# RoPE attention and SiLU FFN on one core: the same 2671 parts in another issue order, 516 of them on another engine

## The chip, the cores and the metric

The kernel runs on one core of a Trainium2 chip. The metric is device time in microseconds (us) from launch to end. Before the change three runs took 667.82, 668.82 and 671.1 us, a median of 668.82 us.

## What is computed

Attention over 4 batches, 8 heads, 576 positions and head size 64, with a rotation of q and k by position (RoPE), and a feed-forward network (FFN) on its output, 2304 tokens wide 512, inner width 2048. All inputs are 32-bit floats. Cut to what matters:

```python
q_rot, k_rot = rotate(q), rotate(k)
scores = 1 / sqrt(64) * q_rot @ k_rot.T
attn = exp(scores - max(scores)); attn /= sum(attn) + 1e-9
x = (attn @ v), heads side by side          # 2304 x 512
h = x @ w_in                                # 512 -> 2048
out = (h * sigmoid(h)) @ w_out              # 2048 -> 512
```

## The kernel before, in words

Matmuls run on TensorE (PE) with 16-bit operands. A 32-bit number is held as a high and a low half: the high half is the number times a scale, rounded to 16 bits; the low half is what that rounding left over. So nearly every tensor is made twice on the other engines: a "hi" step (one multiplication; L327 on ScalarE, called ACT, or L321 on VectorE, called DVE, and GpSimd, called POOL) and a "lo" step. On DVE a lo step is one fused instruction (L333); on POOL it is two, a multiplication (L321) and a subtraction (L336). POOL can take neither a score nor any other tile that PE writes, since those lie in PSUM; all its work is between tiles in SBUF.

The work comes in named parts, each a few instructions on one engine:

- For each batch b and pair of heads p: loads of q, k and v (`qld`, `vld`), a scale for each from its sum of squares (`qtr`, `qtd`, `qmm` and `sc0` to `sc2`), three rotation steps for q and for k (`rope`: L471, L475, L478), their halves (`qhi`, `qlo`), the transposes by DMA (`qT`), a copy of K with the halves swapped (`ksw`), and the halves of v (`vhi`, `vlo`).
- For each of 8 slices of the weights: two loads (`wld`), a rewriting of the bits (`wT`, `wC` and `wX`, L651 to L664), a scale (`wtr`, `wtd`, `wmm`), and halves (`whi`, `wlo`).
- For each of 144 slots, a slot being 128 query rows against 576 keys of one head: scores on PE (`S`, L778 and L784, into one of 2 PSUM buffers), the row maximum on DVE (`max`), the exponential on ACT (`exp`, L810), the reciprocal of the row sum (`nr0`, `nr1`), the halves of the probabilities (`hi`, `lo`, written to a tile named `pn`), and a transpose by DMA (`T`, L836). The maximum has two forms: a reduction (L799) with a small negation behind it (`neg`, L805 on ACT or L321 on DVE), or a fused form on DVE (L794 with a read of its accumulator), which needs no negation.
- For each unit (half of a batch's query rows, 8 units) and pair: probabilities times v on PE (`pv`, L875), whose result becomes the halves of the FFN's input (`xh`, `xl`, L893).
- For each unit and weight slice: the first FFN matmuls (`m1`, 24 matmuls, L929), tanh on ACT (L941; L939 in the last), a fused add and multiply on DVE (`g`, L945), halves (`gh`, `gl`), and twice 6 second matmuls (`m2`, L985). The last FFN unit, `rem`, has the query rows left over by the others.

Each part has a list of the engines that it may run on. Nothing else decides the order: a table named `ORDER` (L38 to L168) lists all 2671 parts by number with a letter for the engine (t is PE, a ACT, d DVE, D the fused maximum on DVE, p POOL, s the queue of DMA issues on SyncE, called SP, A a DMA issue from ACT). The program walks it once, and each engine's instructions stand in the order of the walk:

```python
with tc.manual_schedule():
    for z, e in re.findall(r"(\d+)(\w)", ORDER):
        pl.run(pl.names[int(z)], e)
```

The engines work through their own instructions strictly in that order; semaphores make one wait for another. The number of buffers is fixed: three each for the exponentials (`e`), the halves of the probabilities (`pn`) and the FFN inputs (`xh`, `xl`), two for scores, one for `m1` and for `g`, two for `gh` and `gl`.

The two helpers that make the halves, with the choice of engine:

```python
def part_hi(e, hi, src, s):
    if e is act: act.activation(hi, src, AF.Copy, scale=s)
    else: times(e, hi, src, s, 1.0)
def part_lo(e, lo, src, s, hi):
    if e is dve: dve.scalar_tensor_tensor(out=lo, in0=src, scalar=s, in1=hi, op0=ALU.mult, op1=ALU.subtract)
    else:
        times(e, src, src, s, 1.0)
        e.tensor_tensor(out=lo, in0=src, in1=hi, op=ALU.subtract)
```

Of the kernel before, what the change touches and what calls it, by code (L numbers as in the profile page):

```python
# [38 lines left out]
1s 4s 5t 21d 3s 2s 38s 0d 72s 540s 544s 7t 39t 6d 41t 22d 8d 9t 10d 11d 23p 75t 55p 15p 42d 56p 40d 16d 57d 76d 83d  # L39
73t 43t 84d 13d 542a 541a 543d 44d 545a 74d 546p 547d 45d 17p 77t 550t 551d 46d 28s 12d 18p 29t 24a 58d 30d 19d 31t  # L40
96s 130s 78d 79d 80d 32d 49p 33d 20s 50p 62s 47d 25d 51d 26s 34d 89p 90d 548t 97t 98d 549d 85d 552t 553d 27A 59p 52d
53d 35a 99t 100d 36d 54s 86a 87d 63t 106s 61A 131t 101d 744t 91d 37d 14d 60s 102d 560s 92p 745D 753t 64d 93d 132d 754d
133t 134d 746a 103p 747a 748a 88s 749d 755a 105d 756a 735t 736D 48d 65t 117d 554d 66d 135d 109t 107t 140t 555d 750a
110d 108d 141d 136d 751d 752s 564s 762t 737a 738a 763d 739a 556a 764d 104d 765a 766a 94s 586s 123d 740d 741a 767d 557d
111t 757a 758d 771t 118p 772D 742d 137a 119p 112d 773d 138d 113d 562a 774a 558a 142t 789t 143d 114d 759p 120p 790d
124d 81d 115d 760d 566p 125p 780t 568s 561a 791d 792a 743s 781D 768d 769d 559d 144d 67d 563d 798t 799d 782d 770s 139d
68d 565a 567d 775a 126a 587a 127d 116d 569a 783a 784d 570a 761s 606s 571d 69a 70d 800d 793a 794d 785d 786a 95A 121d
787d 574t 572t 776d 777p 795a 788s 147s 573d 575d 576t 122s 577d 801a 796d 71d 578d 579d 807t 580a 778d 2031t 590s
797s 802d 803d 128s 129s 82d 808D 581d 809d 582p 810a 811d 825t 145d 583d 162p 826D 804a 805d 827d 146d 588a 607a 816t
817d 828a 829a 812d 818a 819a 813p 592a 148a 830d 156d 589d 2032d 2033d 814d 834t 806s 779s 835d 820a 591a 630s 608a  # L50
609d 836a 149a 852t 150t 157d 610s 837a 831a 593d 151d 163p 821d 152d 832d 853D 854d 838a 839d 584d 632a 833s 843t
822p 823p 844D 153d 855a 724d 2034t 612a 164d 611a 634s 824s 594t 595d 158p 631a 159p 596t 597d 840d 598t 599d 154d
600d 626s 613d 845a 846a 861t 862d 635a 165a 636a 847a 841d 842s 614t 615d 633d 178s 616t 637d 848d 617d 863a 2035a
864a 618t 849a 856a 585d 815s 627a 160p 850d 601d 865d 619d 620d 857d 870t 871D 640t 851s 858p 628a 187p 629d 859d
2036d 872d 638t 602a 873a 874a 875d 621d 866d 641d 639d 604a 876a 867a 603d 642t 643d 644d 868d 860s 645d 622a 646a
877p 897t 898d 605d 648p 899a 647d 900a 869s 650a 878s 879t 2037t 880d 915t 651d 2038a 881a 882a 672s 888t 623d 901a
883a 624a 884d 2039d 2040t 885p 916D 917d 918a 902d 625d 2041d 906t 919a 889D 920d 903a 652s 674a 2042d 886p 166p 890d
904d 891a 892d 921a 893d 887s 161s 656s 907D 908a 2127t 924t 925D 2128a 909a 2129d 653a 2130a 926d 922d 725d 654a 905s
# [12 lines left out]
1051D 1052d 2165d 697d 1030p 2170d 1053a 1035a 1054a 1021p 1041t 1042d 1036a 720a 2047a 1037d 1059t 1031s 1055d 1043d
176d 2171t 200s 2048d 1038a 718a 2174a 1039d 2049t 1044a 1045a 1056a 1060d 2175d 719d 1022s 1040s 1086t 721p 2176a
1061d 177d 240s 2180t 1046d 1047p 1048p 1057d 2177d 1062a 2050a 201a 1063a 2163d 1058s 1087d 722a 1068t 1064d 1065a
1088d 2172t 1089a 2051d 2181a 202t 1069D 1070d 1071a 1090a 217d 723d 203d 2182d 2178t 1072d 2179t 1104t 204d 727d
1091d 1073d 205d 230A 255p 2183p 1077t 1049s 229s 249d 1078d 206a 241a 207d 1066d 1079d 2052t 1067s 2184p 2185t 208d
231s 1074a 1092a 2053a 1093d 2054d 1105d 1094s 242a 1080a 1075d 2186d 1106a 1107a 2191t 2192a 1081d 1108d 2188t 2193d
250p 1095t 1082d 1076s 2194a 243t 244d 1096D 1097a 1083d 1098a 1113t 2198t 2195d 251p 1109d 245d 246d 252a 1084d 256p
257d 2199a 2200d 2196t 1140t 2189d 1141d 1114D 1085s 258a 1115a 259d 253p 2205t 232a 2187s 233t 234d 2201a 254s 1116a
1099a 1117d 1118d 728d 247d 235d 1100d 1101p 1142d 2202d 1110a 1111d 2197t 1131t 2203t 2204t 236d 1102d 2206a 1143a
2207d 1119d 1122t 262s 2208a 1132D 263a 237p 238d 1133d 1134a 1123d 1120d 1124a 1135d 2212t 239d 1144d 1149t 1136d  # L80
264t 2209p 265d 1150D 1145d 266d 1125a 1126a 260s 1112s 1103s 261A 1137p 2210t 271t 1138d 2211t 272d 1127d 1121s 1128d
273t 274d 2213a 1158t 1151d 2214d 1159D 275d 1129p 1160d 276d 1152a 2055t 1153d 248d 2215d 277d 2216d 1154d 1146a
# [1005 lines left out]
```

## Time and profile before

| what | us |
|---|---|
| median of three runs | 668.82 |
| the profiled execution | 666.31 |
| its span, first to last instruction | 664.5 |
| PE busy | 580.1 (87%) |
| DVE busy | 511.5 (77%) |
| ACT busy | 392.0 (59%) |
| POOL busy | 332.9 (50%) |

A busy time is the time in which at least one instruction of the engine ran. The shares are means over stages that differ: the first 200 us, in which inputs and weights are made ready beside the first slots, and the rest, in which slots and FFN matmuls alternate. The 1.8 us between the profiled time and the span lie before the first and after the last instruction.

### The profile page before, as it was taken

The page shows a single profiled execution, that of the slowest core. Times are in us where ns is not written, and L with a number is a line of the kernel's source. Part 1 is how long each engine was busy: PE and PEld are TensorE (multiplying, and loading weights), DVE is VectorE, ACT ScalarE, POOL GpSimd, SP SyncE. Part 2 cuts the span into 40 slices and gives each one's busy share as a digit, 9 for nine tenths or more (in the row PEclk, how much of TensorE's full clock was granted, in tenths as well). Part 3 has the DMA queues.
Part 4 walks back from the last instruction along what each step waited for, and adds up shares of the span by engine and source line. Part 5 has one row for each costly group of instructions (what it writes and reads, how often), then busy time and mean ns, then how long its engine had stood idle before and what let it go on. Part 6 is the DMA issues. An engine that isn't in the chain of part 4 may idle for free. (4 is left out here: it accounts for less than half of the span.)

```text
span 664.5 us, 12551 instructions
## 1 busy us (share of the span) xinstructions
PE 580.1 (87%) x4428; PEld 382.8 (58%) x4428; DVE 511.5 (77%) x1201; ACT 392.0 (59%) x817; POOL 332.9 (50%) x288
## 2 busy tenths in 40 slices
PE   3463668797889899899989989999999999999997
PEld 2331345564556576656666656666666666666663
DVE  5899999999998989889869889888778976322112
ACT  2156778888877676667774765755556554112322
POOL 4532347346755566833657547746555365231220
PEclk9999766989989999999998999999999999999999
DMA  9799989997898949899994799896865775200201
GB/s 313 144 200 277 250 253 210 193 231 200 144 164 157 181 88 175 146 164 187 167 197 88 124 163 179 157 153 125 181 119 106 89 128 113 53 17 0 49 1 33
DMA packets 233327, 98.34 MB, mean 148 GB/s; under 512 B 214192, under 2 KB 214448, under 8 KB 233264
## 3 DMA queue, kind: packets, MB, share of 16 engines
q1 hardware_dynamic: 232144, 95.47, 72.1%
q10 hardware_dynamic: 1120, 2.07, 1.4%
q8 instruction: 35, 0.57, 0.4%
q14 instruction: 28, 0.23, 0.1%
HBM read 36.16 MB, written 4.72 MB: 62 GB/s over the span
## 5 line engine op out<-in xcount | busy, mean ns | idle before, releaser
L929 PEld LDWEIGHTS <-w_in 128*128 128x128 f16 x1728 | 166.4, 98 | 37.9 <-issue 8.1
L929 PE MATMUL m<-xh,w_in 128*128 128x256 f16 x1024 | 178.7, 273 | 3.2 <-DVE g L945 3.0
L985 PE MATMUL m<-w_out,gh 128*128 128x512 f16 x576 | 173.4, 383 | 0.0
L810 ACT ACTIVATE e<-s,small 128x576 f32<-128x576 f32 x144 | 111.7, 775 | 59.3 <-DVE s L794 15.3
L929 PE MATMUL m<-xl,w_in 128*128 128x256 f16 x512 | 139.5, 273 | 2.1 <-DVE xl L893 2.0
L778 PE MATMUL s<-Tk,Tq 128*128 128x512 f16 (+1 forms) x512 | 90.6, 306 | 26.3 <-ACT e L810 19.6
L985 PE MATMUL m<-w_out,gl 128*128 128x512 f16 x288 | 110.4, 383 | 1.1 <-DVE small L819 0.4
L333 DVE SCALAR_TENSOR_TENSOR pn<-e,small,pn 128x576 f16<-128x576 f32 x105 | 97.2, 926 | 8.6 <-POOL pn L321 4.3
L945 DVE SCALAR_TENSOR_TENSOR g<-g,m 128x512 f32<-128x512 f32 x72 | 49.1, 682 | 70.9 <-ACT g L941 39.4
L985 PEld LDWEIGHTS <-gh 128*128 128x128 f16 x576 | 53.2, 100 | 53.9 <-issue 4.1
L321 POOL TENSOR_SCALAR pn<-e,small 128x576 f16<-128x576 f32 x43 | 40.4, 940 | 83.7 <-DVE small L824 37.4
L941 ACT ACTIVATE g<-m,small 128x512 f32<-128x512 f32 x64 | 43.7, 683 | 62.3 <-PE m L929 50.8
L778 PEld LDWEIGHTS <-Tq 128*128 128x128 f16 x512 | 42.1, 105 | 65.6 <-issue 33.1
L327 ACT ACTIVATE pn<-e,small 128x576 f16<-128x576 f32 x77 | 59.0, 769 | 29.0 <-DVE small L824 11.3
L875 PE MATMUL pv<-pt,vh 128*64 128x256 f16 (+1 forms) x576 | 68.8, 307 | 4.0 <-DMA pt<-pn 2.7
L794 DVE TENSOR_SCALAR_CACHE_REDUCE s<-s,small 128x576 f32<-128x576 f32 x82 | 66.5, 814 | 4.2 <-PE s L778 3.0
L321 POOL TENSOR_SCALAR g<-g,small 128x512 f32<-128x512 f32 x30 | 24.8, 826 | 64.9 <-DVE gh L321 30.7
L336 POOL TENSOR_TENSOR pn<-e,pn 128x576 f16<-128x576 f32 x39 | 55.6, 1425 | 3.3
L985 PEld LDWEIGHTS <-gl 128*128 128x128 f16 x288 | 28.3, 98 | 38.4 <-DVE gl L333 4.0
L875 PEld LDWEIGHTS <-vh 128*64 128x64 f16 x576 | 39.7, 118 | 15.0 <-issue 10.9
L321 POOL TENSOR_SCALAR e<-e,small 128x576 f32<-128x576 f32 x39 | 35.5, 910 | 25.6 <-ACT pn L327 18.7
L799 DVE TENSOR_REDUCE small<-s 128x1 f32<-128x576 f32 x62 | 46.1, 745 | 1.2 <-PE s L778 0.9
(145 smaller groups left out, 933.4 us busy)
## 6 DMA issues: line engine op xcount, KB each, us to landing
out_dram<-ob SPq DMA_DIRECT2D x36, 128.0 KB, 2.5
w_in<-in_moe_w_in_dram SPq DMA_DIRECT2D x4, 1024.0 KB, 6.4
w_out<-in_moe_w_out_dram SPq DMA_DIRECT2D x4, 1024.0 KB, 6.8
io<-in_v_dram SPq DMA_DIRECT2D x13, 288.0 KB, 4.0
io<-in_q_dram SPq DMA_DIRECT2D x13, 288.0 KB, 3.4
io<-in_k_dram SPq DMA_DIRECT2D x13, 288.0 KB, 3.7
io<-in_v_dram SPq DMA_DIRECT2D x13, 256.0 KB, 4.4
ring<-in_moe_w_in_dram SPq DMA_DIRECT2D x3, 1024.0 KB, 7.1
```

Of the source, the lines that this page charges most:

```text
L321: e.tensor_scalar(out=out, in0=in0, scalar1=s1, scalar2=s2, op0=ALU.mult, op1=ALU.bypass if s2 is None else ALU.mult)
L327: act.activation(hi, src, AF.Copy, scale=s)
L333: dve.scalar_tensor_tensor(out=lo, in0=src, scalar=s, in1=hi, op0=ALU.mult, op1=ALU.subtract)
L336: e.tensor_tensor(out=lo, in0=src, in1=hi, op=ALU.subtract)
L778: pe.matmul(o, tq[:, j, 2 * c:2 * c + 2, :], kt[:, r0:r1, js], start=(n == 0), stop=(n == 1))
L794: dve.tensor_scalar(out=t, in0=t, scalar1=cc[:, 1:2], scalar2=None, op0=ALU.mult, op1=ALU.min, accum_out=m_of(1, 2),)
L799: dve.reduce_max(out=m_of(0, 1), in_=buf("s", i)[:, 0:S], axis=AX.X)
L810: act.activation(buf("e", i), buf("s", i)[:, 0:S], AF.Exp, bias=m_of(1, 2), scale=-1.0 if fused[i] else cc[:, 0:1], accum_out=m_of(2, 3),)
L875: pe.matmul(o[64 * j:64 * j + 64, 0:m], vt[part][:, j, s, :], pt[:, a, j, 0:m], start=(z == 0), stop=(z == len(steps) - 1),)
L929: pe.matmul(t[:, c, 0:n], w[:, wz, kk, fs], xx[:, kk, 0:n], start=(kk == 0 and x == 0), stop=(kk == KD - 1 and x == 2),)
L945: dve.scalar_tensor_tensor(out=g, in0=g, scalar=1.0, in1=t, op0=ALU.add, op1=ALU.mult)
L985: pe.matmul(o, gs[gz][:, c, ts], w[:, wz, c], start=(first and c == 0 and x == 0), stop=(last and c == 1 and x == 2),)
```

## The change

Only the table `ORDER` changes. The parts, their code, their tiles and buffers are the same. Its first line, as an example:

```diff
-1s 4s 5t 21d 3s 2s 38s 0d 72s 540s 544s 7t 39t 6d 41t 22d 8d 9t 10d 11d 23p 75t 55p 15p 42d 56p 40d 16d 57d 76d 83d
...
+45d 50p 55d 545a 12d 73t 74d 18a 24a 19d 51p 75t 83d 25p 541a 29t 30d 76d 542a 77t 56d 78d 79d 20s 47d 13d 46d 96s 57d
```

On PE the sequence of parts keeps its pattern and changes by a few places here and there. Over the whole program 516 parts run on another engine than before. What that sums to, in numbers of parts:

| part | before | after |
|---|---|---|
| `lo` of the slots, DVE / POOL | 105 / 39 | 95 / 49 |
| `qlo`, DVE / POOL | 25 / 7 | 21 / 11 |
| `gh`, ACT / DVE / POOL | 35 / 23 / 14 | 38 / 15 / 19 |
| `gl`, DVE / POOL | 42 / 30 | 41 / 31 |
| `rope`, DVE / POOL | 42 / 54 | 47 / 49 |
| `vhi`, ACT / DVE / POOL | 10 / 2 / 4 | 5 / 7 / 4 |
| `whi`, ACT / DVE / POOL | 17 / 1 / 2 | 19 / 0 / 1 |
| maximum, reduction / fused | 62 / 82 | 50 / 94 |
| `nr0`, ACT / DVE | 84 / 60 | 75 / 69 |
| `ksw`, issued by ACT / SP | 7 / 9 | 3 / 13 |

The first place is on POOL, in the preparation of batch 0, whose q, k and v lie for the time being in the weights' tiles `w_in` and `w_out` (and whose halves lie in `n` or `w_out`). Before:

```order
L478 TENSOR_TENSOR w_in<-w_in,rt 128x576
L321 TENSOR_SCALAR n<-w_in,small 128x9x64
L471 TENSOR_TENSOR rt<-w_out,sin_t 128x576
L475 TENSOR_TENSOR w_out<-w_out,cos_t 128x576
L471 TENSOR_TENSOR rt<-w_in,sin_t 128x576
L321 TENSOR_SCALAR w_out<-w_out,small 128x576
L336 TENSOR_TENSOR w_out<-w_out 128x9x64
L321 TENSOR_SCALAR w_out<-w_in,small 128x9x64
L321 TENSOR_SCALAR vh<-w_in,small 128x1152
```

And after, on the same engine, from the fifth instruction of the preparation on:

```order
L321 TENSOR_SCALAR w_in<-w_in,small 128x576
L336 TENSOR_TENSOR n<-w_in,n 128x9x64
L321 TENSOR_SCALAR w_out<-w_out,small 128x576
L336 TENSOR_TENSOR w_out<-w_out 128x9x64
L471 TENSOR_TENSOR rt<-w_in,sin_t 128x576
L475 TENSOR_TENSOR w_in<-w_in,cos_t 128x576
L478 TENSOR_TENSOR w_in<-w_in,rt 128x576
L471 TENSOR_TENSOR rt<-io,sin_t 128x576
L321 TENSOR_SCALAR vh<-w_in,small 128x1152
L321 TENSOR_SCALAR w_in<-w_in,small 128x576
L336 TENSOR_TENSOR w_out<-w_in,w_out 128x9x64
```

Where POOL had one low half (the L321 and L336 in a row), it now has three in this stretch and a fourth right behind it; the two single L321 on `n` and `w_out`, high halves, have gone to ACT.

The second place is on DVE, around the low half of the FFN input of unit 1's last pair (`xl`, L893), for which the first FFN matmul of unit 1 waits. Before:

```order
L799 TENSOR_REDUCE small<-s 128x1
L333 SCALAR_TENSOR_TENSOR vl_130<-io,small,vh 128x320
L333 SCALAR_TENSOR_TENSOR pn<-e,small,pn 128x576
L321 TENSOR_SCALAR small<-small 128x1
L333 SCALAR_TENSOR_TENSOR vl_130<-io,small,vh 128x320
L333 SCALAR_TENSOR_TENSOR pn<-e,small,pn 128x576
L893 SCALAR_TENSOR_TENSOR xl<-pv,small,xh 128x256
L893 SCALAR_TENSOR_TENSOR x_rem_122<-pv,small,x_rem_121 128x64
L799 TENSOR_REDUCE small<-s 128x1
L333 SCALAR_TENSOR_TENSOR pn<-e,small,pn 128x576
```

And after:

```order
L333 SCALAR_TENSOR_TENSOR vl_130<-io,small,vh 128x320
L824 RECIPROCAL small<-small 128x1 x2
L794 TENSOR_SCALAR s,small<-s,small 128x576
L333 SCALAR_TENSOR_TENSOR pn<-e,small,pn 128x576
L333 SCALAR_TENSOR_TENSOR vl_130<-io,small,vh 128x320
L893 SCALAR_TENSOR_TENSOR xl<-pv,small,xh 128x256
L893 SCALAR_TENSOR_TENSOR x_rem_122<-pv,small,x_rem_121 128x64
L794 TENSOR_SCALAR s,small<-s,small 128x576
L819 TENSOR_SCALAR small<-small 128x1
```

Both reductions (L799) have become fused maxima (L794), the negation between them is gone, and one low half of the probabilities (`pn`) fewer stands ahead of `xl`.

## Rows read from the trace of the kernel before

**Rows 1.** The page: the span, and each engine's busy time, share and instructions.

```profile
span 664.5 us, 12551 instructions
PE 580.1 (87%) x4428; PEld 382.8 (58%) x4428; DVE 511.5 (77%) x1201; ACT 392.0 (59%) x817; POOL 332.9 (50%) x288
```

**Rows 2.** Windows: busy time by engine in five stretches, clock, DMA share.

```profile
core 0: us, PE busy (x) PEld busy (x) DVE busy (x) ACT busy (x) POOL busy (x), PEclk, DMA share, GB/s
0.00:25.00 25.00, 10.04 (x65) 7.53 (x66) 16.04 (x36) 5.35 (x5) 11.69 (x13) 1.00 0.79 246
25.00:114.20 89.20, 52.50 (x325) 33.59 (x325) 82.81 (x204) 61.38 (x110) 39.94 (x32) 0.83 1.01 230
114.20:199.80 85.60, 71.71 (x550) 47.41 (x549) 80.91 (x191) 72.25 (x143) 48.21 (x39) 0.96 0.93 190
199.80:572.70 372.90, 359.24 (x2905) 237.05 (x2904) 308.85 (x736) 231.36 (x511) 213.21 (x184) 1.00 0.79 143
572.70:664.50 91.80, 86.57 (x589) 57.26 (x588) 22.87 (x38) 21.70 (x50) 19.89 (x22) 0.99 0.09 21
```

**Rows 3.** Waits of DVE, then of PE, from 25 to 200 us.

```profile
DVE junk L350 <- PE s L346: 2.0, 3, 1.2
DVE xl L893 <- ACT x_rem L327: 1.5, 1, 1.5
...
PE s L778 <- ACT e L810: 15.6, 11, 3.1
PE s L688 <- DVE junk L350: 9.8, 7, 4.7
```

**Rows 4.** Waits of PE from 200 to 573 us.

```profile
PE s L778 <- ACT e L810: 4.0, 5, 1.9
PE m L929 <- DVE g L945: 3.0, 5, 0.7
PE m L929 <- DVE xl L893: 1.6, 3, 0.8
```

**Rows 5.** Instructions by shape until 199.8 us: count, busy us, mean ns of one.

```profile
L333 DVE SCALAR_TENSOR_TENSOR pn<-e,small,pn 128x576 f16<-128x576 f32 x28 | 24.5, 876 | 0.4 <-ACT pn L327 0.2
L794 DVE TENSOR_SCALAR_CACHE_REDUCE s<-s,small 128x576 f32<-128x576 f32 x21 | 17.0, 815 | 0.5 <-PE s L778 0.2
L799 DVE TENSOR_REDUCE small<-s 128x1 f32<-128x576 f32 x20 | 14.9, 745 | 0.0
L333 DVE SCALAR_TENSOR_TENSOR n<-io,small,n 128x576 f16<-128x576 f32 x6 | 4.8, 818 | 0.0
L321 DVE TENSOR_SCALAR small<-small 128x1 f32<-128x1 f32 x26 | 4.7, 188 | 0.1
L333 DVE SCALAR_TENSOR_TENSOR gl<-g,small,gh 128x512 f16<-128x512 f32 x5 | 4.2, 837 | 0.0
L794 DVE DVE_READ_ACCUMULATOR s<-s,small 128x1 f32 x21 | 2.9, 140 | 0.0
L336 POOL TENSOR_TENSOR pn<-e,pn 128x576 f16<-128x576 f32 x10 | 15.4, 1536 | 0.8
L321 POOL TENSOR_SCALAR e<-e,small 128x576 f32<-128x576 f32 x10 | 10.2, 1022 | 5.3 <-ACT pn L327 5.0
```

**Rows 6.** Instructions by shape, whole span: a high half on DVE.

```profile
L321 DVE TENSOR_SCALAR pn<-e,small 128x576 f16<-128x576 f32 x24 | 15.8, 660 | 2.9 <-DMA pt<-pn 2.5
```

**Rows 7.** Timeline of POOL and DVE: start, duration, instruction.

```profile
22.68 1.41 POOL L471 TENSOR_TENSOR rt<-w_out,sin_t 128x576 f32<-128x576 f32 x1
22.75 1.95 DVE L333 SCALAR_TENSOR_TENSOR n<-w_in,small,n 128x576 f16<-128x576 f32 x1
...
206.86 0.80 DVE L333 SCALAR_TENSOR_TENSOR pn<-e,small,pn 128x576 f16<-128x576 f32 x1
```

**Rows 8.** The chain that ended last: start, duration, what.

```profile
574.33 1.69 PE m L929 x14
...
651.54 2.63 PE m L929 x24
```

More of the change, by code (lines that the diff above doesn't have):

```diff
@@ L44 @@
[L44 to L58, printed above, removed]
@@ new lines @@
+150t 151d 152d 157d 816t 817d 813a 154d 818d 592a 591a 593d 814p 819a 820d 821d 843t 831a 844d 822p 158p 153d 165a
+845a 832d 852t 632a 833s 823d 634s 846a 824s 2034t 853d 581d 631a 633d 159p 611a 854a 612a 840a 594t 595d 596t 597d
+598t 724d 599d 160d 626s 847a 848d 849p 600d 614t 613d 615d 855a 856d 841d 601d 861t 862D 616t 604a 617d 850p 636p
+863a 815s 618t 864a 635a 585d 870t 637d 619d 842s 640t 851s 857d 858p 628a 627a 620d 871D 629d 872a 641d 859d 860s
+873a 621d 602a 638t 874a 875d 865a 866d 639d 642t 603d 897t 2035a 876a 643d 2036d 644d 867a 868d 155d 645d 622a 646a
@@ new lines @@
+1449a 2301a 2302d 2076t 1413a 384d 2077a 2078d 2303a 1409s 2311t 1414d 1424d 2187s 2304d 1415d 1416d 2312a 2313d 363a
+389p 1437t 1383t 1438d 1417d 1384D 390p 2305t 2306a 364t 365d 1385d 2314d 1450d 366d 1439a 1386a 1387a 2315d 393s
+2318t 1425p 1451d 1452d 2319a 2320d 367d 368d 2316t 1388d 1426p 370d 2308t 1427s 394a 402t 1453p 385s 1418s 1440a
+1441d 1428t 1464t 403d 1442d 369d 2325t 404t 1429D 1430a 1431a 1443p 1444p 1389p 1454s 378d 1465d 2321a 1473t 405d
+2322d 2309a 409s 1466a 1467a 2326a 1390p 1474D 1432d 1468d 1433d 2327d 1469d 1470a 395t 2317t 2323t 406d 391s 1482t
@@ new lines @@
+2367s 2430s 1841s 2474a 1844a 1845a 1821d 1887t 1888D 1885d 2109t 2110a 1860t 2471t 2475d 1822p 1823s 2472t 1886s
+1846d 1847d 2476a 1889d 1890a 1861d 1862a 1863a 1864a 2111d 2477d 1891d 1892d 733d 2478t 1851t 1848d 1893p 1849d 1852D
+1853d 1854a 1894p 1869t 1870d 1865d 2480t 2481a 1959t 1850s 1866d 2479t 1960D 1871a 1872a 1855a 2482d 1895s 2483a
+1867d 1856d 1961a 1857d 1962a 2112t 1963d 1873d 1858p 1874d 1875a 1964d 1859s 2113d 2114d 1905t 1923t 1924D 1925a
+2491t 1926a 1906D 1868s 2484p 1896t 2485t 2492a 1876d 2493d 2494d 1907a 2495p 1897D 1927d 1928d 1908a 2488t 1909d
@@ new lines @@
+1929d 2498t 1877s 2489d 1968t 1965a 2115t 1966p 1898d 2499a 2500d 1899a 1900a 1930d 1932t 1910d 1969D 1911a 2486a
+1970d 1912p 1967s 1971a 1933D 1901d 1902d 1934d 2505t 2501a 1935a 1914t 1950t 1931s 1913s 1936d 2502d 1915D 1903d
+1951D 1916d 2506a 2496t 1917a 1918a 1919d 2497t 1920a 2507d 2503t 2004t 2508a 1952d 2509d 1937d 2512t 2504t 1921p
+1904s 1938a 1953a 2005D 1954d 2513a 1955d 2006d 2514d 1922s 2307s 1939d 1940s 1956a 1957d 1941t 1972d 1958s 2515d
+2516d 1973d 2007a 2519t 1986t 2510t 1942D 2116d 1987D 1943d 1974a 1988d 1944a 1975d 1976s 2511t 1945d 2520a 2521d
@@ new lines @@
+1989a 1990a 2117d 1946d 1991d 1992p 2522a 1993d 2008d 1947p 2523p 2517t 2118t 2022t 2023D 1977t 1978D 1979d 1980a
+1948p 1981a 2119d 1994s 2487s 1949s 1982d 1983p 2526t 2009d 2527a 2024a 2010d 2528d 1984d 1995t 1996D 2025a 2518t
+2011p 2524t 2013t 2529d 2530p 1985s 2014D 2120d 2026d 1997d 2015d 2533t 2016a 2525t 2017d 2018d 734d 2019d 1998a 1999a
+2000d 2001p 2531t 2012s 2027d 2534a 2535d 2020d 2002p 2536p 2028a 2021s 2537p 2540t 2029d 2030s 2541a 2003s 2121t
+2532t 2538t 2542d 2122d 2123d 2539t 2124t 2125d 2543a 2126d 2544d 2551t 2545t 2552a 2553d 2554a 2548t 2558t 2546d
@@ new lines @@
+2549d 2555d 2550s 2559a 2556t 2560d 2561a 2562p 2557t 2565t 2563t 2564t 2566a 2567d 2568p 2572t 2569d 2570t 2573a
+2574d 2575d 2576d 2571t 2579t 2577t 2580a 2578t 2581d 2582d 2586t 2583p 2587a 2588d 2589d 2584t 2590p 2585t 2593t
+2591t 2594a 2595d 2596a 2597p 2592t 2600t 2601a 2598t 2602d 2599t 2611t 2603p 2604d 2605t 2612a 2608t 2606a 2609a
+2613d 2618t 2614d 2615d 2619a 2616t 2620d 2617t 2547s 2621a 2622p 2625t 2623t 2626a 2624t 2627d 2628d 2632t 2629d
+2633a 2634d 2630t 2631t 2639t 2635p 2636p 2637t 2638t 2640a 2641d 2646t 2642a 2643d 2644t 2647a 2648d 2607s 2610s
@@ L168 @@
+2645t 2653t 2649p 2650p 2490s 2651t 2654a 2655d 2652t 2660t 2656d 2657p 2661a 2662d 2658t 2659t 2663d 2664d 2665t
+2668t 2666a 2667s 2669a 2670s
 """
```

209 lines of the change are left out of this document (96 added, 113 removed).

## The prediction, made before the run

> **What bounds the kernel now.** I read the span and busy times first [rows 1], then the windows [rows 2]. They cut the span into stages with different limits. PE is busy for 580.1 of 664.5 us, but unevenly: 52.5 of the 89.2 us between 25 and 114.2, 71.7 of the next 85.6, and then 359.2 of the 372.9 us up to 572.7. I chose the cuts: at 114.2 the first FFN matmul of unit 0 starts, at 199.8 that of unit 1, at 572.7 that of unit 7.
>
> The reader is to see that another engine is full where PE is not. From 25 to 199.8 DVE is busy for 82.81 + 80.91 = 163.7 of 174.8 us, so it stands still for 11.1. Its waits in this stretch are the longest ones shown and many shorter, none over 1.5 us [rows 3]. PE in the same stretch waits for ACT's exponentials (15.6 us) and for DVE's `junk`, the sums for the scales (9.8). The exponential itself needs the maximum that DVE makes. So the first 200 us are DVE's, and an instruction taken off DVE there moves everything behind it forward.
>
> From 199.8 on it is PE's: 13.7 us of standstill in 372.9 [rows 2], made of many small waits, 4.0 us for exponentials and 3.0 for `g` the largest [rows 4]. DVE has 64.0 us free there and POOL 159.7. From 574.33 to 654.18 the chain that ended last is PE matmul behind PE matmul [rows 8]. Nothing that the change moves shortens the matmuls, so this end is as long as before.
>
> **The change part by part.** I counted the parts in both tables ahead of unit 1's first FFN matmul, the mark at 199.8, and leave out parts that merely moved behind it (among those a `rope` step and an `o` of DVE).
>
> Low halves. DVE makes two `lo` and four `qlo` fewer, as at the first place shown. By the stage's own rows a `lo` is 0.876 us and a `qlo` 0.818 [rows 5]: 2 x 0.876 + 4 x 0.818 = 5.0 us off. One `gl` fewer: 0.837. On POOL each of these is two instructions, 1.022 + 1.536 = 2.56 us [rows 5], so seven of them are 17.9 us.
>
> High halves. DVE loses two `hi`, a `qhi`, a `whi` and an `xh` and gains a `vhi`: net four, for which I take the row of a `hi`, 0.660 us [rows 6]: 2.6 off. They go mostly to ACT, which is busy for 61.38 and 72.25 us in the two stretches of 89.2 and 85.6 [rows 2]: the gaps take four such instructions.
>
> Maxima. Six more are fused, as at the second place shown: 0.815 + 0.140 in place of 0.745 [rows 5], so 6 x 0.21 = 1.3 on. Five negations of DVE go, 5 x 0.188 = 0.9 off, and six `nr0` come, which have no row of their own in my list; at the price of a negation, an upper bound for a column of one element, 6 x 0.188 = 1.1 on. Together 1.5 on.
>
> Sum on DVE up to the mark: -5.0 - 0.8 - 2.6 + 1.5 = -6.9 us. About six sevenths of it are already ahead of the first FFN matmul at 114.2, since three of the four `qlo` and most of the high halves belong to batch 0.
>
> What POOL's new work costs DVE. POOL gets 17.9 us and gives back about 4 (three high halves and two rotation steps net, at 0.7 to 1.9 each), so +14. The timeline has the price [rows 7]: a `qlo` on DVE that started 0.07 us after a POOL instruction took 1.95 us, and the same shape with POOL standing still 0.80. The lower bound of this term is zero, if the new POOL work meets DVE instructions that read one operand from PSUM (the fused maximum's mean is 815 with POOL busy for half the stage [rows 2, 5]). The upper bound is that all of it blocks. The mean says how often it happens: 28 `lo` at 0.876 rather than 0.80 are 2.1 us lost, and if DVE's other instructions between SBUF tiles, some three times as many us by the same view, lose alike, 8 to 9 us for the 99.8 us that POOL is busy until the mark [rows 2]. I take 0.09 us per us of POOL: 14 x 0.09 = 1.3 us on.
>
> This is where a page of the Trainium skill speaks against the change. SBUF — State Buffer, section "SBUF: two separate sides", says that DVE and GpSimd share a pair of ports under an exclusive lock: a DVE instruction with two SBUF inputs and a GpSimd instruction do not share, the later one waits for the whole of the other. The single instruction in rows 7 agrees (1.95 us). The mean of 0.876 does not show it as the rule. By the rule taken for every overlap, the term would be about half of 14, some 7 us, and the gain gone; that is a rival below.
>
> Waiting. DVE stands still for 11.1 us in this stage. With less to do it will be found waiting more: for exponentials, for POOL's results, for loads (the DMA engines' share is 1.01 and 0.93 there [rows 2]). No row shows how much; the ends are no growth and all of the 5.6 us that are left. I take the end near none, 0.6 us, because its waits for DMA are not among the long ones in rows 3. So unit 1's first FFN matmul comes 6.9 - 1.3 - 0.6 = 5 us earlier, and by the same sum unit 0's about 4 to 5.
>
> Behind the mark. DVE makes eight `lo` and eight `gh` fewer there, but four `vhi` and six rotation steps more, and six more of its maxima are fused; by my count its work falls by some 2 us, and POOL's grows by about 19, which at 0.09 takes those 2 back. PE's order has the same pattern. PE there loses 13.7 us of 372.9; slots that come in a slightly other order will change which of its small waits occur, and I have no reason to expect a sign. I add 1 us of gain: PE ran at a granted clock of 0.96 from 114.2 to 199.8 and 0.83 before [rows 2], that is, partly at the 1.2 GHz level, in stretches in which it was mostly waiting for DVE; with the DVE work ahead of it shorter, 0.04 x 71.7 = 2.9 us of PE time are there to win, and I take a third.
>
> So the profiled execution, 666.31 us (span 664.5 and 1.8 around it), becomes 660.3. It lay 2.5 us under the median of the three runs, 668.82. The same 6 us from the median give 662.8 us.
>
> **The rivals.**
>
> No change to speak of. The 7 us that DVE is relieved of come back as blocking by POOL (14 us x the half of DVE's time that is in instructions between SBUF tiles = 7) or as waits in the place of work. For it: the 1.95 us, and that a POOL pair takes 2.56 us where DVE took 0.88, so a result is ready later even when DVE is not blocked. Against it: the mean of 0.876, and POOL at 88 of 175 us in the stage. Time: 667 to 669.
>
> Slower. From 199.8 on POOL becomes the late engine. It gets some 19 us on top of 213.21 of 372.9, 62%. There are 102 slots in this stretch, one every 3.66 us; a slot whose halves are both made on POOL holds it for some 3.6 us (a multiplication of that size at 1.02, and the pair at 2.56 [rows 5]), so two such slots in a row, or one behind a `gl`, already make the third `pn` buffer late, the next exponential waits, and with it PE's next score. It decides where PE's waits for exponentials, 4.0 us now [rows 4], become the largest by far. If PE's standstill doubles, 13.7 us come on and the 6 go off: 668.82 + 7.7 = 676.5. Against it: PE issues the scores well ahead of the products that need them, and only 10 of 144 `lo` move.
>
> More gain. DVE's relief comes through whole, 6.9 us, all of the 2.9 us of clock, and a part of PE's 13.7 us of small waits, say 2: about 12, so 657. For it: the relief is ahead of the first FFN matmul, and PE then starts its dense part with a better-filled queue. Against it: it needs three things at once.
>
> **How the numbers follow.** The forecast, 3.4 to 9 us of gain, gets 0.50; more gain 0.12; no change 0.22; slower 0.16. Half a per cent, about what a measurement of this kernel can tell from none, is 3.3 us: faster 0.50 + 0.12 = 0.62, same 0.22, slower 0.16. The forecast's own range is 660 to 665.5. The wide one goes down to 656, where the clock and the small waits have given all that I found, and up to 673, half way into the slower rival: some 0.05 stay below it and 0.1 above.
>
> **What would show it.** Unit 0's first FFN matmul starts at about 109.5 us and unit 1's at about 195; DVE's busy time falls by 5 to 11 us over the span (its parts sum to some 9 us less, blocking gives some back), POOL's rises by 25 to 35. PE's standstill between unit 1's and unit 7's first matmul stays between 10 and 18 us, and the time from the latter to the end is 91 to 92. The mean of a `lo` on DVE until the mark stays under 0.92. I am wrong in the stage if unit 1's mark is not earlier by at least 3 us; wrong in the price of POOL if that mean passes 0.95; and wrong behind the mark if it is earlier but PE's standstill eats it.

## The result and the profile after

The changed kernel takes 650.03 us (median of four executions, 648.94 to 653.66) against 668.36 for the kernel before, timed beside it: ratio 0.9727, interval 0.9679 to 0.9775. The forecast was 662.8 us with a range down to 656. The sign was right; the gain, 18 us, is three times the 6 that were worked out. Executions more than 1.5% above the fastest of their kernel are in no ratio, though in the medians: below, one of `a3_sequence` (1195.26 us), one of `g1_four_pn_old` (664.61) and one of the kernel before (1992.91).

The profiled execution of after is the slowest of its four, 653.66 us; a second profile of the same kernel, the experiment `a1_again`, is an ordinary one, 650.15 us. I use both.

The page of after, where [rows 1] stood for before (busy us, share of the span, instructions):

```profile
span 651.9 us, 12595 instructions
PE 575.2 (88%) x4428; PEld 378.2 (58%) x4428; DVE 510.4 (78%) x1203; ACT 385.1 (59%) x801; POOL 362.7 (56%) x317
```

POOL's busy time is up by 29.8 us, inside the 25 to 35 forecast. DVE's fell by 1.1 us only, not by 5 to 11. A reader who stops here finds no reason for 12 us.

The windows, with the cuts at the same events as in [rows 2] (first FFN matmul of unit 0, of unit 1, of unit 7). After:

```profile
core 0: us, PE busy (x) PEld busy (x) DVE busy (x) ACT busy (x) POOL busy (x), PEclk, DMA share, GB/s
0.00:25.00 25.00, 10.18 (x64) 7.35 (x64) 14.92 (x40) 8.51 (x9) 11.69 (x12) 1.00 0.99 268
25.00:111.90 86.90, 50.53 (x325) 32.05 (x326) 81.61 (x199) 59.57 (x106) 51.40 (x39) 0.86 0.98 226
111.90:192.40 80.50, 70.70 (x551) 46.42 (x550) 75.73 (x186) 71.32 (x141) 48.68 (x42) 0.98 0.97 194
192.40:560.20 367.80, 357.22 (x2906) 235.10 (x2905) 314.47 (x744) 224.73 (x499) 233.45 (x207) 1.00 0.81 148
560.20:651.90 91.70, 86.56 (x590) 57.23 (x588) 23.64 (x38) 20.98 (x49) 17.53 (x20) 0.99 0.09 21
```

Unit 1's mark comes at 192.4 in place of 199.8. DVE's busy time up to it is 172.3 us in place of 179.8: 7.5 less, and the mark is 7.4 earlier. So close a match is partly luck: six traces with the part of the table up to the mark as before (before, b1, b5, c2, f1, g3) have the mark at 196.2 to 203.0 us and DVE busy for 175.4 to 179.9, five with the changed one (after, a1_again, a4, b4, c1) at 189.7 to 192.4 and 171.4 to 173.2. By their means the mark is 8.4 us earlier; 5.9 of that are DVE's work and 2.5 its standstill. Behind the mark another 5.1 us go (372.9 to 367.8), although DVE works there 5.6 us more than before. Of these 5.1, PE's standstill gives 3.1 (13.7 to 10.6) and its busy time 2.0 (359.2 to 357.2). The last stretch is unchanged, as forecast; the chain there is PE behind PE, as in [rows 8]:

```profile
560.23 2.85 PE m L929 x24
563.08 2.59 PE m L985 x12
...
638.61 2.63 PE m L929 x24
644.63 2.35 PE m L985 x10
```

Most of the 5.1 us lie in one part of the long stretch. I cut it at unit 4's first FFN matmul. Before:

```profile
199.80:391.40 191.60, 182.83 (x1472) 119.95 (x1471) 166.11 (x396) 129.82 (x286) 111.79 (x94) 0.99 0.84 154
391.40:572.70 181.30, 176.41 (x1434) 117.10 (x1434) 142.75 (x340) 101.54 (x226) 101.42 (x90) 1.00 0.73 133
```

The same of the second profile of after:

```profile
190.60:376.00 185.40, 178.31 (x1460) 117.95 (x1459) 171.34 (x394) 122.26 (x276) 130.14 (x112) 1.00 0.89 163
376.00:556.70 180.70, 177.44 (x1447) 116.81 (x1446) 144.79 (x350) 102.80 (x224) 103.50 (x96) 1.00 0.74 135
```

In units 1 to 3 DVE is busy for 5.2 us more and stands still for 14.1 us rather than 25.5, and the stretch is 6.2 us shorter. Some 2 us of that may go with the clock: the granted clock of the stretch is 0.99 before and 1.00 in this second profile, and in the first profile of after, at 0.99 as well, the stretch is 4.2 us shorter (187.4). In units 4 to 6 almost nothing changes. DVE's waits in units 1 to 3 are many and short; its longest group, for POOL's high half, nearly goes. One step upstream are POOL and ACT, whose next write to a `pn` buffer waits until the transpose (`pt<-pn`, a DMA) has read the old one. These waits in units 1 to 3 (us in total, times, longest), before:

```profile
DVE pn L333 <- POOL pn L321: 3.9, 4, 2.2
POOL pn L321 <- DMA pt<-pn: 9.9, 5, 4.3
ACT pn L327 <- DMA pt<-pn: 6.4, 4, 3.2
```

and in the second profile of after:

```profile
DVE pn L333 <- POOL pn L321: 0.2, 1, 0.2
POOL pn L321 <- DMA pt<-pn: 3.2, 1, 3.2
ACT pn L327 <- DMA pt<-pn: 0.9, 2, 0.6
```

One of them in the timeline of before (start, duration, instruction, the idle time before it with its releaser):

```profile
331.77 1.68 POOL L336 TENSOR_TENSOR pn<-e,pn 128x576 f16<-128x576 f32 x1
...
333.48 3.24 SPq L836 DMA_TRANSPOSE pt<-pn  x2
...
337.72 0.75 POOL L321 TENSOR_SCALAR pn<-e,small 128x576 f16<-128x576 f32 x1 [4.27 <-DMA pt<-pn]
...
338.62 1.12 DVE L333 SCALAR_TENSOR_TENSOR pn<-e,small,pn 128x576 f16<-128x576 f32 x1
...
339.86 0.83 ACT L810 ACTIVATE e<-s,small 128x576 f32<-128x576 f32 x1 [0.25 <-DVE pn L333]
```

POOL's own low half of another slot ends at 333.45, that slot's transpose is issued at 333.48 and lands 4.05 us later (at 337.53 by the trace). POOL stands still for 4.27 us, DVE's low half follows POOL's high half, and the next exponential waits for that low half. How little of a wait can reach DVE shows here too: DVE has other work meanwhile, and then stands still for 1.07 us, for this exponential.

Over these stretches of all runs but a2 and a3, in us (before and after are the two profiles; the labels are those of the experiments below). The last column adds the waits of ACT and POOL for a `pn` buffer in units 1 to 3:

| run | to unit 0 | unit 0 | units 1 to 3 | units 4 to 6 | rest | `pn` waits |
|---|---|---|---|---|---|---|
| before | 114.2 | 85.6 | 191.6 | 181.3 | 91.8 | 16.3 |
| after | 111.9 | 80.5 | 187.4 | 180.4 | 91.7 | 3.1 |
| a1_again | 112.0 | 78.6 | 185.4 | 180.7 | 91.7 | 4.1 |
| a4 | 111.0 | 81.0 | 195.7 | 181.5 | 91.8 | 14.9 |
| b1 | 117.5 | 85.5 | 185.6 | 180.9 | 91.5 | 2.7 |
| f1 | 112.2 | 85.8 | 187.2 | 183.4 | 91.8 | 1.1 |
| d3 | 114.5 | 82.4 | 184.8 | 180.4 | 91.5 | 3.1 |
| e1 | 111.3 | 81.7 | 186.4 | 181.4 | 91.7 | 3.2 |
| b2 | 118.1 | 90.6 | 185.5 | 180.7 | 91.7 | 2.5 |
| b4 | 112.3 | 78.8 | 198.9 | 184.0 | 91.6 | 0.3 |
| b5 | 114.8 | 85.8 | 207.2 | 183.8 | 91.8 | 11.1 |
| c1 | 110.4 | 79.3 | 189.1 | 183.8 | 91.4 | 8.2 |
| c2 | 113.8 | 82.4 | 198.7 | 190.0 | 91.8 | 28.0 |
| g1 | 113.7 | 81.5 | 185.5 | 178.7 | 91.7 | 1.3 |
| g2 | 111.7 | 81.0 | 184.0 | 180.3 | 91.7 | 0 |
| g3 | 113.6 | 86.0 | 194.1 | 181.4 | 91.8 | 20.5 |

Leave out b4 and b5, which add DVE work to these units: the others last 184.0 to 189.1 us there where the waits are 8.2 us or less, and 191.6 to 198.7 where they are 14.9 or more. That alone is no proof: the first group has the changed order in these units, the second the old one, and only g1 has the old order without the waits.

### The profile page after: what moved, and what is told of

Same layout as the page of the kernel before. It is cut to its first block, busy times and chain, and to the rows that moved or that the text cites. A ratio compares the mean times of both kernels' runs of the same rounds, so it can differ in the third digit from the quotient of the medians.

```text
span 651.9 us, 12595 instructions
## 1 busy us (share of the span) xinstructions
PE 575.2 (88%) x4428; PEld 378.2 (58%) x4428; DVE 510.4 (78%) x1203; ACT 385.1 (59%) x801; POOL 362.7 (56%) x317
## 5 line engine op out<-in xcount | busy, mean ns | idle before, releaser
L810 ACT ACTIVATE e<-s,small 128x576 f32<-128x576 f32 x144 | 110.5, 767 | 80.5 <-DVE s L794 29.4
L333 DVE SCALAR_TENSOR_TENSOR pn<-e,small,pn 128x576 f16<-128x576 f32 x95 | 93.9, 991 | 13.1 <-ACT pn L327 6.4
L794 DVE TENSOR_SCALAR_CACHE_REDUCE s<-s,small 128x576 f32<-128x576 f32 x94 | 76.1, 814 | 5.5 <-PE s L778 4.6
L321 POOL TENSOR_SCALAR pn<-e,small 128x576 f16<-128x576 f32 x43 | 40.9, 952 | 68.6 <-DVE small L824 35.3
L321 POOL TENSOR_SCALAR e<-e,small 128x576 f32<-128x576 f32 x49 | 45.3, 924 | 52.4 <-DVE pn L321 22.3
L336 POOL TENSOR_TENSOR pn<-e,pn 128x576 f16<-128x576 f32 x49 | 69.9, 1426 | 4.1
L875 PE MATMUL pv<-pt,vh 128*64 128x256 f16 (+1 forms) x576 | 65.1, 298 | 2.4 <-DVE xl L893 2.0
L321 POOL TENSOR_SCALAR g<-g,small 128x512 f32<-128x512 f32 x31 | 23.2, 750 | 54.2 <-ACT gh L327 33.7
L875 PEld LDWEIGHTS <-vh 128*64 128x64 f16 x576 | 36.1, 114 | 14.2 <-issue 10.8
L875 PE MATMUL pv<-pt,vl 128*64 128x256 f16 (+1 forms) x320 | 43.4, 297 | 0.0
```

The source lines that it names most:

```text
L321: e.tensor_scalar(out=out, in0=in0, scalar1=s1, scalar2=s2, op0=ALU.mult, op1=ALU.bypass if s2 is None else ALU.mult)
L794: dve.tensor_scalar(out=t, in0=t, scalar1=cc[:, 1:2], scalar2=None, op0=ALU.mult, op1=ALU.min, accum_out=m_of(1, 2),)
L810: act.activation(buf("e", i), buf("s", i)[:, 0:S], AF.Exp, bias=m_of(1, 2), scale=-1.0 if fused[i] else cc[:, 0:1], accum_out=m_of(2, 3),)
L875: pe.matmul(o[64 * j:64 * j + 64, 0:m], vt[part][:, j, s, :], pt[:, a, j, 0:m], start=(z == 0), stop=(z == len(steps) - 1),)
```

## Experiments

Ratios are against the kernel before, run on the same chip beside each; its median there was between 666.42 and 668.36 us. Fillers and added loads do work whose result nothing reads.

**The whole change again, and its two halves apart.** `a1_again` is after, unchanged. `a2_engines` keeps the order of before with the engines of after, `a3_sequence` the reverse. Of the 516 letters that differ, 74 are maxima that stay on DVE in the other form, and 67 are negations that the fused form drops in one table or both. The first numbers of a2:

```diff
-9t 10d 11d 23p 75t 55p 15p 42d
+9t 10d 11d 23d 75t 55d 15p 42d
```

> The changed kernel once more, unchanged, for a second trace. The first trace is of an execution of 653.7 us, the other three took 648.9 to 650.8. If the first trace was a late execution, this one ends near 650 and shows in which stretch 3 to 4 us more went: the theory of less DVE work says ahead of unit 1's first FFN matmul (192.4 us in the first trace, 188 to 190 here); the rival, that the gain beyond it is PE's, says behind it (367.8 us from unit 1's to unit 7's first FFN matmul in the first trace, 364 here).

> The order of parts of the kernel before, each part on the engine that the changed kernel has for it. Theory A, less DVE work: most of the gain is here, 652 to 657 us. Rival B, the sequence of the parts: none of it, 665 to 670. Rival C, that an order fits its own engine choices alone: slower than before, over 671.

> The order of parts of the changed kernel, each part on the engine that the kernel before has for it. Theory A: 664 to 670 us, no gain. Rival B: most of the gain, 650 to 656. Rival C: over 671.

Measured: again 650.86 us, ratio 0.9772 (0.9702 to 0.9842). The halves: 748.14 us, ratio 1.1224 (1.1154 to 1.1293), and 747.71, ratio 1.1205 (1.1121 to 1.1288). Each half alone costs 80 us. The pages of a2 and then a3:

```profile
PE 597.2 (80%) x4428; PEld 387.4 (52%) x4428; DVE 517.8 (69%) x1203; ACT 386.4 (52%) x801; POOL 353.1 (47%) x317
```

```profile
PE 596.0 (80%) x4428; PEld 386.4 (52%) x4428; DVE 524.8 (70%) x1201; ACT 390.1 (52%) x817; POOL 323.9 (43%) x288
```

The engines' work is nearly that of before and after, but for PE's busy time, which is 16 to 22 us longer. Most of the time is in waits; the longest of PE, in a2 and then in a3 (19.6 us in before, 8.8 in after, over the whole span):

```profile
PE s L778 <- ACT e L810: 49.2, 35, 5.1
```

```profile
PE s L778 <- ACT e L810: 42.7, 36, 6.5
```

So what engine does a part and where it stands in the order belong together, and a sum of durations per engine, which the prediction was, says nothing of how well they fit.

**The table spliced by place.** `a4_new_until_mark`: the changed table up to unit 1's mark, before's order and engines behind it. `b1_new_after_mark`: the reverse. `f1_new_units_1_to_3`: before's up to the mark, the changed one for units 1 to 3, before's again. All parts stay; only their places and letters are taken from the one table or the other. The first numbers in a4; in b1 and f1 they stay as before:

```diff
-1s 4s 5t 21d 3s 2s 38s 0d 72s 540s 544s 7t
+1s 4s 21d 7t 15p 2s 38s 0d 3s 8d 544s 72s
```

> The changed order and engines for all parts ahead of unit 1's first FFN matmul, those of the kernel before for the rest. The traces of both show 7.4 us gained ahead of this mark and 5.2 behind it. If the two are independent: 660 to 662 us. If the second gain only follows from the first (PE and DVE come into the rest with a better-filled queue): 650 to 654. If the rest alone carries the gain of the timed runs: 665 or more.

> The other splice: order and engines of the kernel before for all parts ahead of unit 1's first FFN matmul, those of the changed kernel for the rest. The first splice took 4.5 us off (661.8 against 666.4 us) of 16. If the gains of the two stretches add: 655 us. If the rest needs the new beginning to gain: 660 or more. The theory of the prediction, that the rest is PE's alone and has nothing to give, says 665 to 667.

> The kernel before until unit 1's first FFN matmul, the changed order and engines from there to unit 4's, and the order and engines before for the rest. If the gain behind the mark lies in units 1 to 3: 659 to 663 us, that stretch 185 to 188 us, as in the run with the whole rest new (659.2). If it needs the new order after unit 4 too: 664 or more.

Measured: 661.84 us, ratio 0.9919 (0.9885 to 0.9952); 659.18, 0.9887 (0.9834 to 0.994); 664.8, 0.9957 (0.9923 to 0.9991). By ratio a4 gains 5 and b1 8 us; the intervals overlap, so which side of the mark brings more is not settled. The two sum to 13 where the whole brings 15 to 18. a4's mark is 7.8 us earlier, but units 1 to 3 then take 195.7 us rather than 191.6: the old order gives part of an early start back. f1 is inconclusive as a split, and in the range that was named for a gain that needs the changed order behind unit 4 too: it has the short units 1 to 3 (187.2 us, `pn` waits of 1.1) but loses 2 us behind the second seam.

**Does DVE set the pace, and where?** Three writes of 112 ns each behind every row maximum, to a tile that nobody reads then: `b2_dve_filler_early` on after in slots 0 to 41, `b4_dve_filler_dense` on after in slots 42 to 103 (units 1 to 3 for the most part), `b5_dve_filler_dense_old` on before in the same slots.

```diff
         pl.run(pl.names[int(z)], e)
+        if pl.names[int(z)][0] == "max" and 42 <= pl.names[int(z)][1] < 104:
+            for _ in range(3):
+                dve.memset(junk[0], 0.0)
```

> The changed kernel with three small memsets on DVE behind each maximum of slots 0 to 41 (ahead of unit 1's first FFN matmul): extra DVE work of some 10 us by an estimate from the 0.165 us of the one memset that the trace of before shows (less if a half-sized one is quicker). If DVE is the bound there: the mark moves from 191 us by nearly all of the DVE time added, and the total by about as much. Rival, that the order's fit and not DVE's load sets the pace: the mark moves by less than a third of it.

> The changed kernel with the same filler behind the maxima of slots 42 to 103, that is between unit 1's first FFN matmul and about unit 4's: about 15 us of DVE work. If PE bounds this stretch, as the prediction says: 0 to 4 us slower than the changed kernel, 650 to 654. If DVE bounds it too: 10 us or more, over 660.

> The kernel before with the same filler in the same slots. If PE bounds the stretch: 666 to 670 us. If the order before is nearer to DVE's bound there than the new one: over 676, and more is lost than in the changed kernel.

The instructions added, in b2 and in b4 (count, busy us, mean ns):

```profile
L1056 DVE MEMSET junk<- 128x64 uint32 x126 | 14.1, 112 | 6.7
```

```profile
L1056 DVE MEMSET junk<- 128x64 uint32 x186 | 20.8, 112 | 9.9
```

Measured: b2 666.88 us, 16 more than after for 14.1 us of filler. b4 667.35, 17 more for 20.8. b5 685.29, 17 more than before. In b2 unit 1's mark is 16 to 18 us later than in the two profiles of after, at 13.4 us of filler ahead of it. If PE alone set the pace behind the mark, the filler of b4 and b5 would have vanished in DVE's 64 us of standstill [rows 2]. It did not. Units 1 to 3 in b4 and then in b5:

```profile
191.10:390.00 198.90, 180.98 (x1461) 118.51 (x1459) 183.46 (x554) 122.24 (x277) 126.94 (x112) 1.00 0.81 152
```

```profile
200.60:407.80 207.20, 183.68 (x1472) 119.14 (x1471) 183.40 (x557) 129.56 (x286) 108.02 (x94) 1.00 0.79 143
```

DVE's standstill there is 15.4 us with the filler and 14.1 without it in after's order, 23.8 and 25.5 in before's. The added work did not fill the gaps; it made the stretch longer, by 11.5 to 13.5 us in b4 for 17.8 us of filler in these units, by 15.6 in b5 for 18.1. The gaps are latency in a chain that DVE is part of, not slack. Two things stay open: the filler stands right behind each maximum, so that load on DVE can't be told from delay at this place of a slot's chain, and no run added work to PE, ACT or POOL, which may be part of the same chain.

**Less load on DVE in two other ways.** `d3_low_halves_back` (on after) gives ten low halves ahead of the mark from POOL back to DVE and four the other way, a net six, as before had them. `e1_nr0_on_act` (on after) moves 41 of the small `nr0` from DVE to ACT, behind their exponential. Of d3, and of e1 the kind of edit:

```diff
-18a 24a 19d 51p 75t 83d 25p 541a
+18a 24a 19d 51p 75t 83d 25d 541a
...
-739d
+739a
```

> The changed kernel, but of the low halves ahead of unit 1's first FFN matmul (lo and qlo) the 14 that run on another engine than before are put back: ten from POOL to DVE, four from DVE to POOL, net six more on DVE. Theory D with the prediction's prices: six low halves are 5 us of DVE work, less about 1 us for POOL's blocking: the mark moves from 191 to 194 to 196, the total to 653 to 656. Rival (POOL's blocking gives all back): 649 to 652. Rival (an order fits its own engines only): over 658.

> The changed kernel with 41 of the first step of the reciprocal (nr0) taken from DVE to ACT and put right behind the exponential that makes their input, for slots ahead of unit 4's first FFN matmul. That takes 41 x 0.143 = 5.9 us off DVE. Theory D: faster, 645 to 649 us. Rival (the order's fit counts more than DVE's load): no gain or slower, 650 or more.

Measured: d3 656.83 us, ratio 0.9833 (0.9796 to 0.9871), 6 to 7 more than after, though its interval overlaps that of `a1_again`; e1 653.5, ratio 0.9777 (0.9736 to 0.9818), 3 more than after's median. d3's mark lies at 196.9, against 192.4 and 190.6 in the two profiles of after, and the stretches behind it are as long as after's: what the six low halves cost, they cost ahead of the mark and for good. But d3's DVE is busy there for only 2 us more (174.1 against 172.3 and 171.8); the rest is standstill. e1 has 41 instructions fewer on DVE, yet DVE's busy time is 512.7 us, not below after's 510.4, and ACT's is up by 8 to 393.0: fewer instructions are no relief by themselves, and the faster kernel that was expected of e1 did not come. Why DVE's busy time did not fall is not settled.

**More load on the DMA engines.** Fifty loads of 288 KB, one behind every second slot's transpose from slot 44 on, on after (`c1_more_dma_new`) and on before (`c2_more_dma_old`).

```diff
+        if pl.names[int(z)][0] == "T" and pl.names[int(z)][1] >= 44 and pl.names[int(z)][1] % 2 == 0:
+            x_n[0] += 1
+            o = 576 * (x_n[0] % 5)
+            sp.dma_start(out=ring.rearrange("p i f -> p (i f)")[:, o:o + 576], in_=k[1, 0:2].rearrange("j (p r) d -> (j p) (r d)", r=NR))
```

> The changed kernel with 50 more loads (288 KB each, one behind every second slot's transpose from slot 44 on, from the SP queue into a tile that is free by then; nothing reads them). Theory D (DVE sets the pace up to unit 4, the DMAs do not): 650 to 653 us, no more than 3 us slower than the changed kernel, and the kernel before under the same load loses as little. Rival R (the new order is better because it stands later DMAs): it loses under 4 us here while the kernel before loses over 8.

> The kernel before with the same 50 loads. Theory D: 667 to 671 us. Rival R: over 675.

Measured: 656.45 us, ratio 0.9837 (0.9796 to 0.9878), and 681.3, ratio 1.0208 (1.0151 to 1.0264). The same loads cost the changed order 6 us and the old one 13: more than was expected of c1 by either view, and for c2 what the rival said. In c2, ACT's and POOL's waits for `pn` buffers in units 1 to 3 grow from 16.3 to 28.0 us, in c1 from 3 or 4 to 8.2.

**A fourth `pn` buffer.** The table stays; `pn` gets four buffers, and `xh` two in place of three, for the room: `g1_four_pn_old` on before, `g2_four_pn_new` on after. `g3_two_xh_old` takes the `xh` buffer alone from before.

```diff
-"pn": (3, [128, 2 * S], F16)
+"pn": (4, [128, 2 * S], F16)
...
-"xh": (3, [128, NP, UT], F16)
+"xh": (2, [128, NP, UT], F16)
```

> The kernel before, its table untouched, with four pn buffers rather than three and, to make room, two xh buffers rather than three. Theory D2 (waits for transposes to empty pn hold ACT and POOL, and through them DVE, in units 1 to 3): 660 to 664 us, most of it between unit 1's and unit 4's first FFN matmul (191.6 us before, 185 to 188 here). Rival (the order as a whole): 666 to 669.

> The changed kernel with four pn and two xh buffers. Theory D2: few waits for pn are left in it (0.9 to 3.1 us for ACT, 3.2 or none for POOL in units 1 to 3), so 647 to 651 us. Rival: 640 to 645, as much as in the kernel before or more. If it is faster, it beats both kernels.

> The control: the kernel before with two xh buffers rather than three and three pn buffers as before. 666 to 670 us if the third xh buffer is not needed; whatever it loses has to be added to what the run with four pn buffers gains.

Measured: g1 655.12 us, ratio 0.9793 (0.9745 to 0.9841), more gain than was expected. g2 648.08, ratio 0.9705 (0.9665 to 0.9746). g3 666.79, ratio 0.9989 (0.996 to 1.0017). One buffer brings 12 to 14 us to the old order, and some 2 to the changed one (the intervals of g2 and after overlap, so these 2 are not settled). POOL's waits for `pn` over the whole span, in before and then in g1:

```profile
POOL pn L321 <- DMA pt<-pn: 30.6, 12, 5.1
```

```profile
POOL pn L321 <- DMA pt<-pn: 2.2, 2, 1.3
```

g1's units 1 to 3 by window, with the same instructions on the same engines as before:

```profile
195.20:380.70 185.50, 180.34 (x1471) 119.33 (x1470) 166.50 (x398) 129.77 (x288) 112.85 (x94) 1.00 0.88 160
```

185.5 us in place of 191.6, DVE's standstill 19.0 in place of 25.5, its work the same. g2 has the lowest median of all.

The waits are no price list, though. g1 also gains 4.1 us in unit 0, where the trace of before has none of these waits, and only 2.6 in units 4 to 6, where before has 18.1 us of them at ACT and POOL. And the changed kernel keeps most of them over the whole span, in its second profile

```profile
POOL pn L321 <- DMA pt<-pn: 22.5, 7, 5.9
```

and 9.8 us at ACT, but g2, which has none, gains some 2 us. So g1 and its control show what the lack of a fourth buffer costs, not which wait costs it.

## Why the prediction was right or wrong

**Where it was wrong: "From 199.8 on it is PE's".** This step failed, and with it the 1 us of gain behind the mark, where 5.1 were measured; for PE's small waits there the prediction had put down nothing, and they gave 3.1 of it. PE's busy time, 359.2 of 372.9 us [rows 2], was read as the proof. It is no floor: in g1, with the same matmuls, PE is busy for 180.3 us of units 1 to 3 rather than 182.8, at a granted clock of 1.00 rather than 0.99. DVE's 64 us of standstill were read as room. b4 and b5 show that the filler finds none in units 1 to 3: 17 of 20.8 us of added DVE work come out at the end, in either order. With that step the kind of gain that the traces point to could not be seen: fewer waits of POOL and ACT for a `pn` buffer, and so a shorter standstill of DVE. The row that should have led to it stood in view: the high half on DVE was idle for 2.5 us before `pt<-pn` [rows 6]. POOL and ACT have 30.6 and 9.0 us of such waits over the span, POOL's the longest of its waits behind the mark; I gave them no price, since neither engine was full. That a fourth buffer, which takes these waits away with the table untouched, is worth 12 to 14 us is shown by g1 and its control g3. That fewer such waits are also how the change gains is not shown, only made likely: in its order they fall from 16.3 to 3 or 4 us in units 1 to 3 and the stretch shrinks by 4 to 6, the fourth buffer then adds only about 2, and added DMA load costs it half. What share of the whole gain this is, and why a4 and b1 sum to less than the whole, stays open.

**Right in kind, short in size: the mark.** Forecast 5 us, measured 7.4 and, in the second profile, 9.2. b2 and d3 show that DVE's load ahead of the mark comes out at the end. Over the traces named with the windows, DVE's work falls by 5.9 us, against 6.9 - 1.3 = 5.6 forecast. The mis-sized term is the waiting: 0.6 us more standstill were forecast, and it is 2.5 less. Through which wait that came is not shown. d3 and b2 have the same from the other side: with more work on DVE its standstill grows too, to 22.8 and 25.5 us ahead of the mark from 20.1 and 18.8 in the two profiles of after. Unit 0's mark moved by 2.3 us, not 4 to 5; most of the gain falls between the two marks.

**The price of POOL: wrong by its own test, nearly right as a sum.** The mean of a `lo` until the mark was to stay under 0.92 us; it is 1.005:

```profile
L333 DVE SCALAR_TENSOR_TENSOR pn<-e,small,pn 128x576 f16<-128x576 f32 x27 | 27.1, 1005 | 0.1
```

Minimum, median and maximum of these 27 (ns): most run unhindered, and two take more than twice that time:

```profile
L333 DVE SCALAR_TENSOR_TENSOR pn<-e,small,pn x27: 792/816/1965, 42.9 to 190.8; 128x576 f16<-128x576 f32 x27
```

27 x (1.005 - 0.876) is 3.5 us lost on this shape. It came back on others of DVE's between SBUF tiles. Before, until 199.8 us:

```profile
L475 DVE TENSOR_TENSOR w_in<-w_in,cos_t 128x576 f32<-128x576 f32 x4 | 5.0, 1250 | 2.4 <-POOL rt L471 2.4
L471 DVE TENSOR_TENSOR rt<-io,sin_t 128x576 f32<-128x576 f32 x5 | 4.7, 935 | 0.0
L475 DVE TENSOR_TENSOR io<-io,cos_t 128x576 f32<-128x576 f32 x5 | 4.2, 850 | 1.3 <-ACT n L446 1.3
```

After, until 192.4:

```profile
L475 DVE TENSOR_TENSOR io<-io,cos_t 128x576 f32<-128x576 f32 x5 | 3.7, 750 | 0.3 <-issue 0.3
L471 DVE TENSOR_TENSOR rt<-io,sin_t 128x576 f32<-128x576 f32 x4 | 3.0, 748 | 0.0
L475 DVE TENSOR_TENSOR w_in<-w_in,cos_t 128x576 f32<-128x576 f32 x2 | 1.5, 752 | 1.0 <-PE m L346 1.0
```

The excess over 0.75 us was 4 x 0.50 + 5 x 0.19 + 5 x 0.10 = 3.4 us in these three and is gone. Blocking had moved to other instructions, and one shape's mean does not measure it. An estimate over all of DVE's instructions up to the mark that began under a running POOL instruction, each less the quick ones of its form, is 19.3 us before and 21.4 and 21.2 in the two profiles of after: some 2 us on, 1.3 were forecast.

Who is held follows from who starts first. Ten of the 27 began while a POOL instruction ran and had more than 0.19 us to go; each ended 0.60 to 0.62 us after that instruction's end. The other 17 took 0.79 to 0.82 us, also those during which POOL began something. Before it was 5 of 28. One of the ten:

```profile
47.51 2.25 POOL L478 TENSOR_TENSOR io<-io,rt 128x576 f32<-128x576 f32 x1
48.42 1.95 DVE L333 SCALAR_TENSOR_TENSOR pn<-e,small,pn 128x576 f16<-128x576 f32 x1
```

The rule of the Trainium skill (SBUF — State Buffer, section "SBUF: two separate sides") is that of a DVE instruction with two SBUF inputs and a GpSimd instruction the later one waits for the whole of the other. All 27 agree with it. What the rival made of it, half of POOL's new time, does not follow: DVE pays only where POOL was first.

**DVE's busy time over the span** fell by 1.1 us, not 5 to 11. Behind the mark I had counted 2 us less, which blocking was to take back; it is 5.6 more. The 68 `lo` there take 985 ns on average against 945 before, which is 2.7 us of it.

**Carrying the profile to the median.** The sum was made on 666.31 us, 2.5 under the median, and I subtracted its gain from the median. The profiled execution of after then lay 3.6 us above its own. So of the 12.8 us between 662.8 and 650.03, 6.6 are the sum's against its own profile (660.3 to 653.66), that is 2.4 at the mark and 4.1 behind it, and the rest is the spread of single executions, which [rows 2] could not tell.

**The rivals.** No change and slower did not happen: POOL took its 30 us without becoming late, and what had been PE's longest wait behind the mark, for exponentials, fell from 4.0 us [rows 4] to 1.5. The slower rival's mechanism exists all the same: in a2 and a3 exactly those waits grow to over 40 us over the whole span, from 19.6 in before. "More gain", 657 us, came nearest, but the early clock is not the reason: g1 ran from 25 to 113.7 us at a granted clock of 0.65, between the levels of 1.2 and 2.4 GHz, and reached its mark 4.6 us before the kernel before, which had 0.83.

## What to carry to other kernels

A PE that is busy for 96% of a stretch, and an engine beside it with 17% of standstill, do not settle who sets the pace: some ten per cent of dummy work on the other engine tells more, and where its standstill stays the same and the stretch grows, the place of that work is on the path. Look for waits on the reuse of a buffer (a write waiting for a DMA that still reads), also on engines that are far from full, before counting work: one more buffer was worth two thirds or more of a whole new order. But a total of waits is no price: 32 us of the same kind were left in the changed kernel, and taking them away brought some 2. An issue order and its engine choices are one thing; judge them together, and not by busy times.

## What was not expected of the hardware

- Two tables that differ only in which of two orders goes with which of two engine choices, with PE's matmuls the same and DVE's and POOL's within some 15 and 40 us, differ by up to 98 us in time (650 and 748 us).
- The same instructions of the early stage, those of before, reached unit 1's mark at 196.2, 198.0, 199.6, 199.8, 200.6 and 203.0 us in c2, f1, g3, before, b5 and b1 (in g3 with one `xh` buffer less), and after's at 189.7 to 192.4 us in c1, a1_again, b4, a4 and after. A difference of less than some 7 us at one mark of one trace says little.
- A transpose takes 3.4 us from issue to landing at the median in before, after and g1 alike, and 3.6 with fifty more loads; what the order and the buffer change is only how many of them somebody waits for.
